# One core, an mLSTM cell and a tanh-shrink layer: fixed instruction order on VectorE and ScalarE, steps placed by their due time

## The chip, the core and the metric

The kernel runs on one core of a Trainium2 chip. TensorE (PE in the profile; its weight loads are PEld) multiplies matrices into PSUM, VectorE (DVE) and ScalarE (ACT) work element by element, GpSimd (POOL) and SyncE (SP) mostly issue DMAs here. Each engine has its own list of instructions, and engines wait for each other by semaphores. The metric is device microseconds of one execution; lower is better.

## The reference

Two blocks in a row, all in float32. The first is an mLSTM cell with batch 4, 8 heads, 768 steps and head size 40; the second is a layer with 320 inputs, 2048 hidden features and 320 outputs.

```python
for t in range(S):
    m_new = np.maximum(f_gate[:, :, t] + m, i_gate[:, :, t])
    f_stab = np.exp(f_gate[:, :, t] + m - m_new)
    i_stab = np.exp(i_gate[:, :, t] - m_new)
    C = f_stab * C + i_stab * outer(v_t, k_t)
    n = f_stab * n + i_stab * k_t
    y[:, :, t] = sigmoid(o_gate[:, :, t]) * (C @ q_t) / max(abs(n . q_t), 1.0)
...
h = x @ w_in
out = (h - np.tanh(h)) @ w_out
```

Here x is y with heads and features joined, 3072 tokens of 320. The two weights come as 64-bit floats and are turned into float32 on the chip.

## The kernel before

**Units.** The cell works on 24 units n of 128 tokens: unit n is chunk c = n // 4 of batch b = n % 4. For a unit, `scores` multiplies keys with queries (PSUM tile ps) and its mask step writes P on VectorE; `prepare` makes the values scaled by the gates (vs), the decayed state, and the sigmoid of o; `inter` and `intra` multiply with state and P into ph; `gate` is five short VectorE operations (den, den, den, o, ys) that divide by the denominator and apply o; `update` multiplies into pc, from which VectorE makes the next state; `turn` transposes ys into px, and ScalarE copies px to xT, the input of the layer. The tiles ph, pc and px of all units take turns in two PSUM banks (`small`, tags b0 and b1); from item 16 or so they share one.

**Pairs and items.** The layer works on groups g of two units (256 tokens) and on eighths p of the hidden features. `up` of a pair (g, p) multiplies xT with w_in and w_rest into one of two PSUM tiles ph_up; `shrink` computes g = h - tanh(h) with a polynomial: on ScalarE z and q, two each, on VectorE four operations gt, of which the first two read ph_up; `down` multiplies gt with w_out into po, and when a run of pairs ends, po is added to a partial sum (part) or becomes the output (ob). For groups 4 to 10 `down_seven` does the same with seven products instead of eight, from sums of gt (s1 to s4, `sums_of_g`) and sums of w_out (wT, `sums_of_weights`), and `put_together` adds the results. The 96 pairs are put in 50 items, two pairs each except four. In item x the program gives: `up` of the item's pairs, then (`halves`) its last third and the scores of a new unit, then `shrink` and the mask steps, then `down` of item x - 1.

**Weights.** `weights` makes of each block of 64-bit weights three steps: `fetch` (a DMA by GpSimd's queue into one of eight buffers w64), `split` (w_e and w_m on VectorE, w_e and w_r on ScalarE) and `join` (three VectorE operations, w_r, w_e and the product that is w_in, w_rest or w_out). Five blocks make one p. The blocks of p = 0 are converted in the prologue by hand. For the others, `due[p]` is the item in which p is first used, less a quarter, with some spacing; `spread_over` lays the blocks of p between due[p-1] and due[p].

**What sets the order.** All matmuls and transposes go through the class `T`, which chains each to the one before, so TensorE follows the program throughout. `Pinned` does the same for VectorE and ScalarE (line 107 issues all their instructions, so the profile shows L107 for them), but only until the prologue ends: `Pinned.on = False` (line 838) leaves `self.last` as it is, and each later instruction is tied only to the last one of the prologue. In the loop over items (line 839) the framework orders VectorE and ScalarE by its own plan, from data dependencies and the order of the program.

**Steps between.** What is not dense work (cell steps, weight steps, the gates of chunks 1 to 5) is laid at points of time, in items, by `spread_over`; `cell_slot` gives the steps of a unit with a cost each, `merge` puts the list of an item between the dense steps. A unit's slot is half an item to 1.5 items wide at the start, about 2.5 from item 7 on. Its last steps are `gate` and `turn` of the unit before; in the single-bank form (`single`) they are `gate`, five pauses, four `update`, four pauses, three `turn` of the same unit, four pauses. The old `merge` takes the list whose share of cost done is smaller:

```python
i = int(done[1] / total[1] < done[0] / total[0])
```

A pause, and `gate`, have the cost 0.

**Gates.** `gates(0, 1)` in the prologue handles chunk 0; `gates(1, NT)` at the start of item 1 handles chunks 1 to 5: a scan and three operations on rows, ten transposes, three matmuls, and exponentials, in one go.

Of the kernel before, what the change touches and what calls it, by code (L numbers as in the profile page):

```python
# [39 lines left out]

# [37 lines left out]
def kernel(  # L78
# [16 lines left out]
    class Pinned:  # L95


        on = True

# [3 lines left out]
        def __getattr__(self, name):  # L103
            method = getattr(self.engine, name)

            def call(*args, **kwargs):
                i = method(*args, **kwargs)  # L107
# [10 lines left out]
    class T:  # L118
# [14 lines left out]
        @classmethod  # L133
        def transpose(cls, *args, **kwargs):
            return cls.keep(nc.tensor.transpose(*args, **kwargs))  # L135

# [147 lines left out]
    def gates(c0, c1, idle):  # L284

        t0, t1, cs, n = c0 * L, c1 * L, slice(c0, c1), c1 - c0
# [11 lines left out]
        cols = []  # L298
        for row in (lf, i_sb):
            p = small([L, NT, BH], "pcol")  # L300
            for c in range(c0, c1):
                T.transpose(p[:, c, :], row[:, c * L:(c + 1) * L], ident[0:BH, 0:BH])
            cols.append(p[:, cs])
        V.tensor_copy(out=lfT[:, cs], in_=cols[0])
        A.activation(out=ei[:, 2, cs], in_=cols[1], func=AF.Exp)
        awake(idle)

        def sums_of(w):
            p = small([w.shape[1], NT, BH], "psum_lf")
# [4 lines left out]
        p = sums_of(upto)  # L314
        V.tensor_single_scalar(inv[:, cs], p, 2 * DEEP, op=OP.max)
        least = sums[:, NG * NP + 2 + (c0 > 0):NG * NP + 3 + (c0 > 0)]
        V.tensor_reduce(out=least, in_=inv[:, cs].rearrange("p c n -> p (c n)"), axis=mybir.AxisListType.X, op=OP.min)
        A.activation(out=inv[:, cs], in_=inv[:, cs], func=AF.Exp, scale=-1.0)
        p = sums_of(after)
        A.activation(out=eS[:, cs], in_=p, func=AF.Exp)  # L320
        awake(idle)
        V.tensor_tensor(out=ei[:, 0, cs], in0=ei[:, 2, cs], in1=inv[:, cs], op=OP.mult)
        V.tensor_tensor(out=ei[:, 1, cs], in0=ei[:, 2, cs], in1=eS[:, cs], op=OP.mult)
        half = sums_of(ones).rearrange("p c (b j two) -> p (c b) two j", two=2, j=HH)
        us = slice(c0 * B, c1 * B)
        A.activation(out=eT[:, us], in_=half[:, :, 1, :], func=AF.Exp)
        A.activation(out=eT[0:D, us], in_=half[0:D, :, 0, :], func=AF.Exp)
        V.tensor_single_scalar(least, least, TINY / DEEP, op=OP.mult)
# [7 lines left out]
    def weights(dst, srcs, queue):  # L336
# [12 lines left out]
        def split():  # L349
            if src.dtype == FP:  # L350
                return
            hi = w["hi"] = w["st"].bitcast(I32).rearrange("p (n two) -> p n two", two=2)[:, :, 1]
            lo = w["st"].bitcast(U32).rearrange("p (n two) -> p n two", two=2)[:, :, 0]
            e, m, r = (conv.tile([128, n], I32, name=name, tag=name, bufs=3)[0:p] for name in ("w_e", "w_m", "w_r"))
            w["e"], w["m"], w["r"] = e, m, r

            V.tensor_single_scalar(e, hi, 0x7FF00000, op=OP.bitwise_and)
            A.activation(out=e, in_=e, func=AF.Relu, scale=8.0, bias=rebias[0:p])

            V.tensor_scalar(out=m, in0=hi, scalar1=0xFFFFF, scalar2=0x41000000, op0=OP.bitwise_and, op1=OP.bitwise_or)  # L360
            A.activation(out=r.bitcast(FP), in_=lo, func=AF.Copy, scale=2.0 ** -52)

        def join():
            if src.dtype == FP:
                return
            e, m, r = w["e"], w["m"].bitcast(FP), w["r"].bitcast(FP)

            V.scalar_tensor_tensor(out=r, in0=m, scalar=-7.0, in1=r, op0=OP.add, op1=OP.add)
            V.scalar_tensor_tensor(out=e, in0=w["hi"], scalar=-(1 << 31), in1=e, op0=OP.bitwise_and, op1=OP.bitwise_or)
            V.tensor_tensor(out=dst, in0=r, in1=e.bitcast(FP), op=OP.mult)  # L370

        return fetch, split, join
# [5 lines left out]
    def convert():  # L378
# [211 lines left out]
    def down_seven(some):  # L590
# [4 lines left out]
        def product(where, a, x, b):  # L595
            bank, block = where
            if g not in pS:
                pS[g] = [ps_o.tile([128, 3, HM], FP, name="pS0", tag="po0"),
# [7 lines left out]
        steps = []  # L606
        for k in range(7):
            for x, (_, p) in enumerate(some):
                even, odd = (w_out[:, 2 * p + i, :].rearrange("p (two n) -> p two n", two=2) for i in range(2))
                a11, a12, a21, a22 = (gT[some][i][:, x, tt * L:(tt + 1) * L] for tt in range(GT) for i in range(2))  # L610
                s1, s2, s3, s4 = (t[:, x] for t in gS[some])
                where, a, b = (
                    ((0, 2), a11, even[:, 0]), ((0, 0), a12, odd[:, 0]), ((2, 1), a22, wT[p][:, 3]),
                    ((1, 1), s3, wT[p][:, 2]), ((1, 0), s1, wT[p][:, 0]), ((0, 1), s2, wT[p][:, 1]),
                    ((2, 0), s4, odd[:, 1]))[k]
# [7 lines left out]
    def put_together(g):  # L623
# [8 lines left out]

        A.copy(out=a, in_=bank[0][:, 2])
        V.tensor_tensor(out=ob[:, 0:5:4], in0=bank[0][:, 0:2], in1=twice(a), op=OP.add)
# [391 lines left out]
```

## Time and profile before

| | |
|---|---|
| median of 3 runs | 679.09 us (677.19 to 679.75) |
| the profiled execution | 679.15 us |
| its span, first to last instruction | 677.4 us |
| TensorE busy | 590.0 us, 3471 instructions |
| VectorE busy | 355.3 us, 888 instructions |
| ScalarE busy | 191.7 us, 483 instructions |
| GpSimd busy | 28.8 us, 60 instructions |
| moved by DMA | 38.23 MB |

The span begins with the first instruction and ends with the last; 1.75 us of the execution lie outside it. A matmul of float32 stands in the trace as two records, so counts of matmuls are twice those of the program. A share of busy time is a mean over stages with different limits. Tile names are those of the program without buffer numbers; "px<-ident,ys" is the transpose of `turn`. In the lists of waits, "PE px <- DVE ys" means that TensorE stood before a transpose into px until VectorE had finished ys: either because it reads ys, or because ys was the last to read the PSUM bank that px takes. A wait is put down to what came last. The granted clock of TensorE is given as a share of full speed.

### The profile page before, as it was taken

The numbers are of one execution on the slowest core, as the hardware profiler recorded it, in microseconds if no ns is written. First come the engines' busy times: TensorE is split into PE (matmuls) and PEld (weight loads), VectorE is DVE, ScalarE is ACT, GpSimd is POOL, SyncE is SP. The second block draws the span as 40 slices with busy tenths as digits, with TensorE's granted clock in tenths as the row PEclk, the third lists the DMA queues.
The fourth block names the chain that finished last, engine by engine and source line by source line (L and its number), as shares of the span: only waits on it lengthen the run. The fifth ranks groups of instructions, "written<-read, shape, count | busy, mean of one in ns | idle before, by whom it ended". The sixth has DMA issues, their size and how long they took to land. (4 is left out here: it accounts for less than half of the span.)

```text
span 677.4 us, 9300 instructions
## 1 busy us (share of the span) xinstructions
PE 590.0 (87%) x3471; PEld 488.9 (72%) x3473; DVE 355.3 (52%) x888; ACT 191.7 (28%) x483; POOL 28.8 (4%) x60
## 2 busy tenths in 40 slices
PE   4974977787989798988998899899989999989996
PEld 2854766575767566766887788688878889878874
DVE  1679878989342623363646346444526345534421
ACT  1342644542212321221331222312223121313321
POOL 2012123100000000000000000000000000000000
PEclk8575676899899989999999799989989899989999
DMA  7644345421110101022111112111100000000000
GB/s 217 191 147 147 102 152 157 135 58 49 30 39 20 40 20 39 21 59 78 59 40 41 38 40 70 38 30 39 30 11 30 1 0 20 1 20 1 19 2 24
DMA packets 40868, 38.23 MB, mean 56 GB/s; under 512 B 3856, under 2 KB 38352, under 8 KB 40816
## 3 DMA queue, kind: packets, MB, share of 16 engines
q1 hardware_dynamic: 33000, 22.82, 11.6%
q0 software_dynamic: 2800, 9.18, 4.5%
q10 hardware_dynamic: 5016, 5.57, 2.4%
q8 instruction: 29, 0.48, 0.3%
q14 instruction: 23, 0.19, 0.1%
HBM read 33.62 MB, written 3.93 MB: 55 GB/s over the span
## 5 line engine op out<-in xcount | busy, mean ns | idle before, releaser
L131 PE MATMUL ph_up<-xT,w_in 128*128 128x256 f32 x768 | 217.5, 412 | 3.2 <-ACT xT L107 3.2
L107 DVE SCALAR_TENSOR_TENSOR gt<-ph_up,z 128x512 f32<-128x512 f32 (+1 forms) x100 | 62.6, 665 | 223.4 <-ACT z L107 223.1
L131 PEld LDWEIGHTS ph_up<-xT,w_in 128*128 128x128 f32 x768 | 142.0, 203 | 18.8 <-ACT xT L107 4.3
L107 ACT ACTIVATE z<-ph_up 128x512 f32<-128x512 f32 (+1 forms) x100 | 57.1, 576 | 271.8 <-issue 137.9
L131 PE MATMUL po<-w_out,gt 128*128 128x320 f32 x320 | 110.5, 469 | 9.5 <-DVE part L107 9.4
L131 PEld LDWEIGHTS ph<-vs,P 128*128 128x128 f32 x384 | 73.7, 219 | 21.1 <-issue 6.2
L131 PEld LDWEIGHTS po<-w_out,gt 128*128 128x128 f32 x320 | 56.9, 201 | 29.7 <-DVE part L107 12.1
L131 PE MATMUL ph<-vs,P 128*128 128x41 f32 x384 | 67.2, 275 | 6.7 <-DVE ys L107 3.7
L107 ACT ACTIVATE q<-z,tiny 128x512 f32<-128x512 f32 (+1 forms) x100 | 64.7, 701 | 0.0
L107 DVE SCALAR_TENSOR_TENSOR gt<-q,gt 128x512 f32<-128x512 f32 (+1 forms) x100 | 62.4, 663 | 0.0
L131 PE MATMUL pS<-wT,s 128*128 128x160 f32 x336 | 60.5, 318 | 0.0
L135 PE MATMUL px<-ident,ys 128*128 128x128 f32 x72 | 20.6, 323 | 43.5 <-DVE ys L107 34.6
L131 PE MATMUL ph_up<-xT,w_rest 64*128 64x256 f32 x384 | 55.5, 406 | 0.0
L131 PEld LDWEIGHTS pS<-wT,s 128*128 128x128 f32 x336 | 51.8, 203 | 0.1
L135 PEld LDWEIGHTS px<-ident,ys 128*128 128x128 f32 x72 | 10.9, 161 | 51.4 <-issue 48.3
L131 PEld LDWEIGHTS ph_up<-xT,w_rest 64*128 64x128 f32 x384 | 33.1, 187 | 14.7 <-issue 11.8
L131 PE MATMUL pS<-w_out,gt 128*128 128x160 f32 x224 | 39.8, 313 | 0.0
L131 PEld LDWEIGHTS ph<-state,q 80*128 80x128 f32 x160 | 30.2, 203 | 7.9 <-ACT xT L107 2.6
L131 PEld LDWEIGHTS pS<-w_out,gt 128*128 128x128 f32 x224 | 31.6, 190 | 4.0 <-issue 3.6
L131 PEld LDWEIGHTS pc<-vs,k 128*80 128x80 f32 x160 | 22.2, 169 | 16.4 <-issue 11.2
L107 DVE TENSOR_TENSOR P<-ps,upto 128x512 f32<-128x512 f32 x48 | 31.6, 684 | 3.4 <-PE ps L131 3.4
L131 PE MATMUL pc<-vs,k 128*80 128x82 f32 x160 | 26.1, 263 | 6.6 <-DVE ys L107 5.6
(92 smaller groups left out, 565.0 us busy)
## 6 DMA issues: line engine op xcount, KB each, us to landing
w<-in_moe_w_out POOLq DMA_DIRECT2D x14, 320.0 KB, 3.3
kz<-in_kT SPq DMA_DIRECT2D x48, 80.0 KB
v<-in_v SPq DMA_DIRECT2D x24, 160.0 KB
k<-in_k SPq DMA_DIRECT2D x24, 160.0 KB
o<-in_o_gate SPq DMA_DIRECT2D x24, 160.0 KB
out<-ob ACTq DMA_DIRECT2D x24, 160.0 KB
qz<-in_qT SPq DMA_DIRECT2D x44, 80.0 KB
q<-in_qT SPq DMA_DIRECT2D x40, 80.0 KB
```

Of the source, the lines that this page charges most:

```text
L107: i = method(*args, **kwargs)
L131: return cls.keep(nc.tensor.matmul(*args, **kwargs))
L135: return cls.keep(nc.tensor.transpose(*args, **kwargs))
```

## The change

VectorE and ScalarE stay pinned in the loop too: each of their instructions is tied to the one before it in the program, so they run in the order of the program. Some operations are then no longer given where their input is started but where it is due: a class `Clock` counts the costs of the steps given so far, `later` holds an operation back until so much has passed, and `need` gives it at once where something depends on it.

- In `shrink`, the four gt are given 0.9 to 3.2 us later, and the sums of g behind them; in `put_together` the additions come 0.5 us behind ScalarE's copy; the DMAs of the output, issued by ScalarE, come 1 or 2 us behind what they send, and are pinned too.
- The conversion of a block becomes fetch, exponent, mantissa, one, sign and product, six single steps that `spread_over` lays one by one; each has the cost 0. In `mantissa` w_r is given before w_m.
- `merge` places a step of an item at its share of the item's dense cost, whatever its own cost.
- `gates` is cut in two: `gate_rows` (scan and three operations), for chunks 1 to 5 now in the prologue behind the scores of unit 2, and `gate_columns`, five steps laid over item 0 from 0.1 to 0.9, with the PSUM banks of po instead of b0 and b1. The loads of these gates move ahead of k and o of the first two units.

```diff
     class Pinned:
-        on = True
...
                 if self.last is not None:
                     tc.add_manual_dep(i.ins, self.last.ins.name, NO_SYNC, reason="order of an engine")
-                if Pinned.on:
-                    self.last = i
+                self.last = i
...
+    class Clock:
+        now, serial, waiting = 0.0, 0, []
+        @classmethod
+        def later(cls, key, wait, step):
+            cls.serial += 1
+            heapq.heappush(cls.waiting, (cls.now + wait, cls.serial, key, step))
+        @classmethod
+        def tick(cls, us):
+            cls.now += us
+            while cls.waiting and cls.waiting[0][0] <= cls.now:
+                heapq.heappop(cls.waiting)[-1]()
+        @classmethod
+        def need(cls, key):
+            while any(entry[2] == key for entry in cls.waiting):
+                heapq.heappop(cls.waiting)[-1]()
...
+    load_gates(later)
     for name in "ko":
         for n in range(2):
             load_unit(n, (name,))
...
-    def gates(c0, c1, idle):
+    def gate_rows(c0, c1):
...
+    def gate_columns(c0, c1, bank):
...
+        return forget, admit, since, until, whole
...
+        def exponent():
+            w["hi"] = w["st"].bitcast(I32).rearrange("p (n two) -> p n two", two=2)[:, :, 1]
+            e = w["e"] = conv.tile([128, n], I32, name="w_e", tag="w_e", bufs=3)[0:p]
+            V.tensor_single_scalar(e, w["hi"], 0x7FF00000, op=OP.bitwise_and)
+            Clock.later(w["st"], 0.6, lambda: A.activation(out=e, in_=e, func=AF.Relu, scale=8.0, bias=rebias[0:p]))
...
         for x in range(len(blocks) + 4):
-            def step(x=x):
-                for late, part in enumerate((0, None, 1, None, 2)):
-                    if part is not None and BLOCK <= x - late < len(blocks):
-                        blocks[x - late][part]()
-            steps.append((1.0, step))
+            block = [blocks[i] if BLOCK <= i < len(blocks) else (lambda: None, (), ()) for i in (x, x - 2, x - 4)]
+            steps.append([block[0][0], *block[2][2], *block[1][1]])
...
             for i in range(2):
-                V.scalar_tensor_tensor(out=gt[i], in0=ph[i], scalar=TINY_POLY[0], in1=z[i], op0=OP.mult, op1=OP.mult)
-            for i in range(2):
-                V.scalar_tensor_tensor(out=gt[i], in0=q[i], scalar=TINY_POLY[2], in1=gt[i], op0=OP.add, op1=OP.mult)
+                Clock.later(some, 0.9 + 0.35 * n * i, lambda i=i: V.scalar_tensor_tensor(
+                    out=gt[i], in0=ph[i], scalar=TINY_POLY[0], in1=z[i], op0=OP.mult, op1=OP.mult))
+                Clock.later(some, 1.0 + 0.75 * n + 0.35 * n * i, lambda i=i: V.scalar_tensor_tensor(
+                    out=gt[i], in0=q[i], scalar=TINY_POLY[2], in1=gt[i], op0=OP.add, op1=OP.mult))
             if some[0][0] in SEVEN:
-                sums_of_g(some)
+                Clock.later(some, 1.01 + 1.1 * n, lambda: sums_of_g(some))
...
     def merge(a, b):
-        total = [sum(cost for cost, _ in x) or 1.0 for x in (a, b)]
-        done, at = [0.0, 0.0], [0, 0]
-        while at[0] < len(a) or at[1] < len(b):
-            i = int(done[1] / total[1] < done[0] / total[0])
...
+        total, done, b = sum(cost for cost, _ in a), 0.0, list(b)
+        for cost, step in a + [(0.0, lambda: None)]:
+            while b and (b[0][0] * total <= done or step is None):
+                _, us, other = b.pop(0)
+                Clock.tick(us)
+                other()
+            Clock.tick(cost)
+            step()
+            done += cost
+        for _, us, other in b:
+            Clock.tick(us)
+            other()
...
     for p in range(1, NP):
-        spread_over(steps[ready[p - 1]:ready[p]], due[p - 1], due[p])
+        spread_over([(0.0, step) for some in steps[ready[p - 1]:ready[p]] for step in some], due[p - 1], due[p])
...
-    load_gates(later)
...
     halves(scores(2))
-    split[3]()
+    gate_rows(1, NT)
+    do(split[3])
...
-    Pinned.on = False
+    spread_over([(0.3, step) for step in gate_columns(1, NT, lambda i, shape: ps_o.tile(shape, FP, name="gate", tag=f"po{i}"))], 0.1, 0.9)
     for x in range(len(items) + LAG):
-        if x == 1:
-            gates(1, NT, 0)
...
-        merge(dense, [(cost, step) for _, cost, step in sorted(work[x], key=lambda w: w[0])])
+        merge(dense, [(at - x, cost, step) for at, cost, step in sorted(work[x], key=lambda w: w[0])])
```

More of the change, by code (lines that the diff above doesn't have):

```diff
@@ L596, in product @@
             bank, block = where
+            if isinstance(a, int):
+                a = gS[some][a][:, x]
             if g not in pS:
+                Clock.need("result")
                 pS[g] = [ps_o.tile([128, 3, HM], FP, name="pS0", tag="po0"),
@@ L604, in product @@
             started[bank] = True
-        steps = []
+        steps = [(0.0, lambda: Clock.need(some))]
         for k in range(7):
@@ L690, in product @@
                 po[tt] = ps_o.tile([128, DM], FP, name="po", tag=f"po{tt}")
+            Clock.need(some)
             T.matmul(po[tt], gT[some][i][:, x, tt * L:(tt + 1) * L], w_out[:, f, :], start=start, stop=stop)
@@ L787, with do @@
     awake(9)
-    gates(0, 1, 2)
+    gate_rows(0, 1)
+    forget, admit, since, until, whole = gate_columns(0, 1, lambda i, shape: small(shape, "gate"))
+    forget()
+    admit()
+    awake(2)
+    since()
+    until()
+    awake(2)
+    whole()
     fetch, split, join = zip(*first)
+    def do(steps):
+        for step in steps:
+            step()
+            Clock.tick(10.0)
     begin(0)
@@ L816 @@
     awake(2)
-    join[1]()
-    split[2]()
+    do(join[1])
+    do(split[2])
     inside(1)
```

136 lines of the change are left out of this document (67 added, 69 removed).

## The prediction, made before the change was run

> **What bounds the kernel now.** I read the busy time of each engine in five stretches first, because the shares of the whole span mix stages with different limits.
>
> ```profile
> span 677.4 us, 9300 instructions
> ```
> ```profile
> core 0: us, PE busy (x) PEld busy (x) DVE busy (x) ACT busy (x) POOL busy (x), PEclk, DMA share, GB/s
> 0.00:38.00 38.00, 26.27 (x139) 18.93 (x141) 17.66 (x61) 8.44 (x22) 6.05 (x19) 0.73 0.66 196
> 38.00:157.00 119.00, 92.57 (x506) 76.56 (x506) 100.81 (x298) 55.21 (x144) 22.76 (x41) 0.76 0.42 126
> 157.00:324.00 167.00, 144.26 (x764) 110.13 (x763) 72.49 (x169) 37.09 (x95) 0.00 (x0) 0.95 0.13 38
> 324.00:661.00 337.00, 316.53 (x2024) 276.46 (x2024) 161.35 (x357) 87.61 (x217) 0.00 (x0) 0.97 0.09 27
> ```
>
> The 38 us at the front are a prologue whose order is already fixed on every engine. From 38 to 157 us VectorE is the fullest engine (100.81 of 119) while TensorE runs at a granted clock of 0.76, so its work is only about 92.57 x 0.76 = 70 us at full speed. From 157 us on TensorE is the bound: 144 of 167 and 317 of 337 us. Next, what TensorE waits for: the waits of that engine alone, one fence each for the second, third and fourth stretch (total, times, longest).
>
> ```profile
> PE px L135 <- DVE ys L107: 16.0, 5, 5.2
> ```
> ```profile
> PE px L135 <- DVE ys L107: 11.9, 4, 4.4
> PE po L131 <- DVE part L107: 8.2, 7, 1.7
> ```
> ```profile
> PE px L135 <- DVE state L107: 8.8, 5, 2.7
> PE px L135 <- DVE ys L107: 6.7, 3, 3.3
> PE pc L131 <- DVE ys L107: 3.7, 3, 2.2
> ```
>
> These are waits for a short result of VectorE, though VectorE is half idle there. The timeline of one of them shows why.
>
> ```profile
> 231.22 1.29 DVE L107 SCALAR_TENSOR_TENSOR gt<-ph_up,z 128x512 f32<-128x512 f32 x2 [2.89 <-ACT z L107]
> ...
> 233.62 1.28 DVE L107 TENSOR_TENSOR P<-ps,upto 128x512 f32<-128x512 f32 x2
> 234.82 0.16 DVE L107 SCALAR_TENSOR_TENSOR den<-ph,inv 128x8 f32<-128x8 f32 x1
> 234.90 0.48 DVE L107 TENSOR_TENSOR part<-po,part 128x320 f32<-128x320 f32 x1
> ...
> 235.36 0.82 DVE L107 TENSOR_TENSOR vs<-v,ei 128x640 f32<-128x640 f32 x1
> ...
> 236.85 0.49 DVE L107 TENSOR_TENSOR ys<-ph,o 128x320 f32<-128x320 f32 x1
> ...
> 237.49 0.45 PE L135 MATMUL px<-ident,ys 128*128 128x128 f32 x1 [4.14 <-DVE ys L107]
> ```
>
> The five operations of `gate` (den to ys) run from 234.82 to 237.34, 2.5 us, of which part and vs, put between them, take 1.3; alone they would take 1.2 us. They begin only behind gt, a second pair of gt and P (231.22 to 234.90); `turn` has been given so close behind that TensorE stands 4.14 us. A stall also costs clock (stretches as above):
>
> ```profile
> 199.70:201.60 1.90, 0.00 (x0) 0.01 (x1) 1.67 (x5) 0.00 (x0) 0.00 (x0) 1.00 0.19 37
> 202.00:205.20 3.20, 3.20 (x9) 2.51 (x8) 0.00 (x0) 0.47 (x1) 0.00 (x0) 0.50 0.17 51
> ```
>
> After 1.9 us of silence TensorE got half its clock for at least 3.2 us. The Trainium skill ("TensorE: Matmul & The Clock Gate", Part 1) puts the return to half speed after an idle window of about 3.4 us; by that, stalls under that length would cost no clock, and the two clock terms below would nearly vanish (13 us less gain). The row speaks against it, and the sum goes by the row.
>
> **The change, part by part.**
>
> (a) *Weight conversion held to its place.* One group of w (five blocks) is an eighth of these rows of VectorE:
>
> ```profile
> L107 DVE SCALAR_TENSOR_TENSOR w_e<-w,w_e 128x256 int32<-128x256 int32 (+2 forms) x40 | 16.6, 414 | 0.0
> L107 DVE SCALAR_TENSOR_TENSOR w_r<-w_m,w_r 128x256 f32<-128x256 f32 (+2 forms) x40 | 16.5, 413 | 0.3 <-ACT w_r L107 0.3
> L107 DVE TENSOR_SCALAR w_e<-w 128x256 int32<-128x256 int32 (+2 forms) x40 | 11.3, 283 | 0.0
> L107 DVE TENSOR_SCALAR w_m<-w 128x256 int32<-128x256 int32 (+2 forms) x40 | 11.3, 282 | 0.0
> L107 DVE TENSOR_TENSOR w_out<-w_r,w_e 128x320 f32<-128x320 f32 x16 | 7.7, 482 | 0.1
> L107 DVE TENSOR_TENSOR w_in<-w_r,w_e 128x256 f32<-128x256 f32 x16 | 6.6, 412 | 0.1
> L107 DVE TENSOR_TENSOR w_rest<-w_r,w_e 128x128 f32<-128x128 f32 x8 | 2.3, 282 | 0.0
> ```
>
> Sum 72.3, a group 9.0 us. The places come from `due`: 0.5, 1.75, 3.75, 5.75, 7.5, 8.75 and 11.75 items for groups 1 to 7. The view of the tile w_out and the groups of VectorE from 38 to 157 us say where they ran:
>
> ```profile
> L107 DVE TENSOR_TENSOR w_out<-w_r,w_e x16: 477/481/493, 38.9 to 156.3; 128x320 f32<-128x320 f32 x16
> ```
> ```profile
> L107 DVE SCALAR_TENSOR_TENSOR gt<-ph_up,z 128x256 f32<-128x256 f32 (+1 forms) x12 | 6.4, 556 | 16.2 <-ACT z L107 16.2
> L107 DVE SCALAR_TENSOR_TENSOR gt<-q,gt 128x256 f32<-128x256 f32 (+1 forms) x12 | 6.3, 555 | 0.0
> ```
>
> The last block is done at 156.3 us, when only six items (12 gt, two an item) have passed: nothing holds VectorE to the program in the loop, and groups 5 to 7 ran up to six items early, in the stage where VectorE is the bound. In program order these 3 x 9.0 = 27 us leave the stretch, whose VectorE work falls to about 73, beside TensorE's 70. What is it then worth? At best the stretch runs at the ratio of now, 119/100.8, over 73: 86 us. At worst VectorE's idle time (16.2 us before gt) only grows and 119 stays. I take the middle, 102: both engines now wait in turn for each other, and half clock will not go. Gain 17 us, less 4 for (d): 13.
>
> The 27 us come back in items 6 to 12. There VectorE has 5 to 7 us of conversion an item beside gt (2.6), its share of the cell (vs, P, state and gate, near 5 us a unit, a unit in 1.5 to 2.5 items) and a part or two, 11 to 13 us, against 10.9 us that an item of the fourth stretch takes (337 us, 31 items); items 6 to 8 are over by some 2 us each. Cost 7 us. The sums of w_out, too, are now held to their place:
>
> ```profile
> L107 DVE TENSOR_TENSOR wT<-w_out 128x160 f32<-128x160 f32 x16 | 4.8, 318 | 0.0
> ```
>
> With the other 16 like them that is 10 us in items 18 to 22, in lumps of four (1.3 us), beside gt and s. From 0 (idle VectorE takes them) to 6 us (half of them in front of something due); I take 2.
>
> (b) *`merge` puts steps where they are due.* The old merge went by cost, so `gate` and the pauses (cost 0) made no distance; now a step stands at its share of the item. From item 19 a unit has 33 steps over about 2.5 items of 10.9 us, 0.8 us a step: six steps, 5 us, from `gate` to the first `update`, five from the last `update` to `turn`. A chain of 1.2 us behind at worst four gt (2.6) fits. Of the 19.2 us of waits in the fourth stretch 17 go, and of its clock loss, (1 - 0.97) x 337 = 10 us, 8. Before that (third stretch) a unit has 20 steps over 2.5 items, and only two, 2.4 us, from the last `intra` to `turn`: of the 11.9 us a third stays, gain 8. The part waits (8.2) come from gt pairs in front of the eviction; spaced, one gt (0.66) at most is in front, and two products (0.54 us each by the program's own cost) cover it: 6. Clock: of (1 - 0.95) x 167 = 8.4 us, 5.
>
> (c) *gt given 0.9 to 3.2 us after the item's end, s behind it; masks P in front.* Cost nothing, as long as gt has read the bank before the next item's first matmul. The chain of waits has the cover:
>
> ```profile
> 618.88 4.00 PE pS L131 x28
> 622.88 4.52 PE ph_up L131 x24
> ```
>
> These 4.0 us of pS, and the cell's products, stand between. P (1.28) and two gt (1.29) need 2.6 of them after the scores. If the cover went, each us late would cost a us an item, 50 items.
>
> (d) *Later gates.* The scan and three operations move into the prologue:
>
> ```profile
> L107 DVE TENSOR_TENSOR_SCAN xT<-xT,xT,xT 32x640 f32<-32x640 f32 x1 | 1.5, 1529 | 0.0
> L107 DVE TENSOR_TENSOR xT<-xT,xT 32x640 f32<-32x640 f32 x3 | 2.4, 809 | 0.0
> ```
>
> 3.9 us of VectorE in front of the conversions that item 0 needs; I count them in full, as nothing there covers them. Leaving item 1 they free the px wait of 5.2 us there (already in (a)). The two loads (32 x 640 x 4 B each, 164 KB, 0.8 us at the 196 GB/s of the first stretch) go ahead of k and o on SP's queue; k's first reader is the first `update`, behind the whole of unit 0, and o is read later still: 0, or 0.8 us if that cover goes. The transposes change banks and place, not count: 0, bounds -1 to +3 for the chain in item 0.
>
> (e) *Fixed order on ScalarE, out DMAs included.* ScalarE is under half full everywhere; -1 to +4, I take 0. The swap of w_m and w_r: 0.
>
> Sum: second stretch 13, third 8 + 6 + 5 - 7 = 12, fourth 17 + 8 - 2 = 23; 48 us. 677.4 - 48 = 629, plus 1.75 outside the span (the profiled execution took 679.15, the median is 679.09): **631 us**.
>
> **Rivals.**
>
> *A, the early stage gives nothing.* VectorE and TensorE work in lockstep at half clock, and what (a) saves returns in items 6 to 8: for it, the clock of 0.76 with TensorE idle only 22%; against it, 27 us less work. Without the 13 us of the second stretch it is 644; with only two thirds of the 44 us of (b) besides, 659.
>
> *B, slower: the wrong thing in front.* With a fixed order a VectorE operation whose input is late stops everything behind it, gt above all, and gt frees the two up banks. Place: between an item's end and the next item's first matmul. Against it: gt needs 2.6 of 4.0 us. It decides once gt is late by 1 us beyond that cover in each of 50 items (50 us against the 48); at 1.4 us it is 679 - 48 + 70 = 701. The Trainium skill says the queues of VectorE and ScalarE are strictly first in, first out ("TensorE: Matmul & The Clock Gate", Part 1, on the engines' queue depths); by that the chip would not repair such an order. The trace of before shows no operation that is late in this way.
>
> *C, the order hardly changes.* If VectorE already runs nearly in program order, 679. The conversions at 156 us speak against it, as does `part` between two `den`.
>
> *D, stalls cost no clock.* If the half clock of the last two stretches comes from something other than the stalls, the 8 and 5 us stay lost: 644. Against it: it follows the silence of 1.90 us directly, and the clock was 1.00 until then. The Trainium skill's idle window, cited above, would come out here.
>
> **Chances.** Forecast (613 to 646) 0.55, A beyond that (to 670) 0.25, D 0.04, C 0.06, B 0.10. The forecast's own ends: (a) at 86 and wT at 0 give 613; (b) at two thirds 646. The range takes in A at two thirds and the unknowns of (d) and (e), and below the forecast's end some 7 us for the 7 of items 6 to 8: 606 to 664. A measurement of this kernel can tell about 0.5% from no change; faster by more than that 0.84, within it 0.06, slower 0.10.
>
> **What would show it.** The last w_out conversion at about item 11 instead of 156 us; VectorE under 80 us in the time of items 0 to 5; no px or pc waits above 1 us after item 19, granted clock 1.00 there; part waits under 2 us in all; pS waiting on wT around items 18 to 22 if (a) costs more. I am wrong if TensorE waits for gt or z, or if items 0 to 8 take as long as before.

## The result, and the profile after

| | median us (range) | ratio to before, 95% interval |
|---|---|---|
| before, 4 runs beside it | 679.35 (677.19 to 679.75) | |
| after, 4 runs | 620.46 (616.0 to 623.15) | 0.9133 [0.9076, 0.9189] |

The change makes the kernel 8.7% faster. The profiled execution of after took 616.0 us, the shortest of its four; the stages below are cut from it, so their sum, 63.1 us, is a little more than the 58.9 between the medians. First the head of the page of after. The counts of instructions are those of before or close to them; TensorE is busy for 25.6 us less, VectorE for 9.4 more.

```profile
span 614.3 us, 9270 instructions
...
PE 564.4 (92%) x3473; PEld 472.7 (77%) x3473; DVE 364.7 (59%) x888; ACT 188.7 (31%) x483; POOL 28.2 (5%) x60
```

To compare stages, both traces are cut at the same work: at the first z of items 0, 5, 18 and 49 (the z that ScalarE takes from an item's first finished `up`), and once more from item 1 to item 5. The windows of before, columns as in the prediction (busy time and count of each engine, granted clock, DMA share, GB/s):

```profile
49.10:149.40 100.30, 77.44 (x432) 64.20 (x432) 86.58 (x256) 47.01 (x120) 20.07 (x36) 0.75 0.41 124
149.40:323.90 174.50, 151.09 (x808) 115.49 (x807) 79.61 (x190) 40.38 (x104) 0.00 (x0) 0.95 0.14 40
323.90:662.60 338.70, 318.23 (x2034) 277.46 (x2035) 161.45 (x357) 87.74 (x218) 0.00 (x0) 0.97 0.09 26
```

The same three of after:

```profile
54.10:137.00 82.90, 67.04 (x418) 55.94 (x418) 54.15 (x150) 28.75 (x77) 9.19 (x17) 0.84 0.33 99
137.00:293.50 156.50, 146.35 (x810) 112.37 (x807) 101.10 (x256) 52.90 (x137) 9.69 (x18) 0.98 0.23 67
293.50:599.40 305.90, 305.90 (x2034) 271.60 (x2035) 176.03 (x386) 88.66 (x225) 0.00 (x0) 1.00 0.10 30
```

Items 0 to 4 take 17.4 us less, items 5 to 17 18.0, items 18 to 48 32.8; the first z comes 5.0 us later. In the last row TensorE is busy for 305.90 of 305.90 us at full clock: there nothing but less work would help. VectorE's 86.58 us in the first row have become 54.15, and the 79.61 in the second 101.10: the conversions moved back. The waits of TensorE over the whole of after (total, times, longest), three rows of the list:

```profile
PE px L133 <- DVE ys L106: 18.7, 9, 3.0
...
PE ph_up L129 <- ACT xT L106: 6.7, 3, 5.6
...
PE po L129 <- DVE part L106: 1.0, 3, 0.4
```

The part waits are down to 1.0 us, and all px waits left lie before item 18. The long wait of ph_up for xT, 5.6 us once, is new. The table gives every profiled execution of this study cut in the same way (us; starts of z in each trace).

| | first z of item 0 | item 0 | items 1-4 | 5-8 | 9-17 | 18-48 | rest | span |
|---|---|---|---|---|---|---|---|---|
| before | 49.1 | 30.9 | 69.4 | 58.6 | 115.9 | 338.7 | 14.9 | 677.4 |
| after | 54.1 | 24.1 | 58.8 | 46.6 | 110.0 | 305.8 | 14.9 | 614.3 |
| e1, loop free | 55.2 | 24.8 | 59.3 | 52.0 | 102.3 | 305.8 | 14.8 | 614.1 |
| e2, old merge | 55.1 | 22.2 | 62.6 | 47.9 | 109.1 | 320.9 | 15.0 | 632.9 |
| e3, before pinned | 48.8 | 31.0 | 71.5 | 63.8 | 119.8 | 368.7 | 14.9 | 718.6 |
| e4, before + merge | 48.0 | 30.7 | 67.0 | 54.4 | 106.7 | 309.3 | 14.8 | 631.0 |
| e5, gt at once | 54.8 | 25.2 | 67.1 | 55.1 | 120.2 | 311.0 | 14.8 | 648.2 |
| e6, blocks whole | 56.6 | 23.1 | 61.9 | 48.4 | 108.6 | 305.8 | 14.9 | 619.3 |
| e7, gates back | 49.1 | 28.6 | 61.0 | 46.6 | 108.2 | 305.8 | 15.2 | 614.5 |
| e8, turn later | 55.7 | 22.3 | 61.3 | 46.1 | 103.1 | 305.8 | 14.9 | 609.4 |
| e9, free, gt at once | 55.2 | 26.3 | 69.6 | 54.0 | 105.9 | 309.3 | 15.1 | 635.4 |
| e10, free, turn later | 54.7 | 24.6 | 59.7 | 44.3 | 101.7 | 305.8 | 15.1 | 605.9 |
| e11, e7 + e8 | 49.4 | 27.9 | 61.3 | 46.1 | 103.1 | 305.8 | 15.1 | 608.6 |
| e12, e11 + other queue | 41.8 | 28.2 | 59.9 | 46.1 | 103.1 | 305.8 | 15.4 | 600.3 |

There is one trace of each kernel, and two runs of one kernel may differ by some us (after's four span 7 us), so single differences of 1 or 2 us in the early columns are not read.

### The profile page after: what moved, and what is told of

Read it like the earlier page. It is cut to its first block, busy times and chain, and to the rows that moved or that the text cites. A ratio compares the mean times of both kernels' runs of the same rounds, so it can differ in the third digit from the quotient of the medians.

```text
span 614.3 us, 9270 instructions
## 1 busy us (share of the span) xinstructions
PE 564.4 (92%) x3473; PEld 472.7 (77%) x3473; DVE 364.7 (59%) x888; ACT 188.7 (31%) x483; POOL 28.2 (5%) x60
## 4 chain that ended last, share of the span: by engine, by line
PE 82%; DVE 12%; DMA 2%; issue 1%; ACT 1%; ACTq 0%; SPq 0%; DVEq 0%
PE ph_up L129 37%; PE pS L129 19%; PE po L129 11%; PE ph L129 8%; PE ps L129 4%; DVE gt L106 2%; PE pc L129 2%; DVE P L106 2%; PE px L133 2%; DMA kz<-in_kT 1%; PE awake L129 1%; DVE o L106 1%; DVE den L106 1%; DVE w_e L106 1%; DVE ys L106 1%
## 5 line engine op out<-in xcount | busy, mean ns | idle before, releaser
L129 PE MATMUL ph_up<-xT,w_in 128*128 128x256 f32 x768 | 206.8, 398 | 6.7 <-ACT xT L106 6.7
L129 PEld LDWEIGHTS ph_up<-xT,w_in 128*128 128x128 f32 x768 | 135.7, 194 | 20.4 <-ACT xT L106 7.2
L129 PE MATMUL po<-w_out,gt 128*128 128x320 f32 x320 | 107.7, 459 | 1.4 <-DVE part L106 1.0
L106 DVE TENSOR_TENSOR P<-ps,upto 128x512 f32<-128x512 f32 x48 | 30.9, 686 | 75.8 <-PE ps L129 75.8
L129 PE MATMUL ph<-vs,P 128*128 128x41 f32 x384 | 65.5, 266 | 6.1 <-DVE vs L106 3.1
L129 PEld LDWEIGHTS po<-w_out,gt 128*128 128x128 f32 x320 | 55.4, 196 | 18.9 <-DVE part L106 3.5
L129 PE MATMUL pS<-wT,s 128*128 128x160 f32 x336 | 56.3, 304 | 0.0
L129 PEld LDWEIGHTS pS<-wT,s 128*128 128x128 f32 x336 | 48.0, 190 | 0.0
L106 ACT ACTIVATE w_e<-w_e,rebias 128x256 int32<-128x256 int32 (+2 forms) x40 | 20.3, 508 | 74.0 <-DVE w_e L106 73.9
L133 PE MATMUL px<-ident,ys 128*128 128x128 f32 x72 | 19.1, 291 | 19.5 <-DVE ys L106 18.7
L129 PEld LDWEIGHTS ph<-state,q 80*128 80x128 f32 x160 | 28.5, 195 | 6.5 <-issue 1.3
L129 PEld LDWEIGHTS ps<-qz,kz 40*128 40x128 f32 x384 | 28.9, 211 | 2.3 <-DVE P L106 0.8
L133 PEld LDWEIGHTS px<-ident,ys 128*128 128x128 f32 x72 | 10.2, 147 | 26.2 <-issue 22.2
```

The costliest lines, as they stand in the source:

```text
L129: return cls.keep(nc.tensor.matmul(*args, **kwargs))
```

## The experiments

Every ratio is to the kernel before, timed beside it, and kernels are compared with each other by these ratios.

**e1: the fixed order taken out of after's loop.** VectorE and ScalarE are pinned to the end of the prologue only; due times, single steps, merge and gates stay.

```diff
+        on = True
...
-                self.last = i
+                if Pinned.on:
+                    self.last = i
...
+    Pinned.on = False
     for x in range(len(items) + LAG):
```

> The changed kernel, but VectorE and ScalarE free in the loop again (tied only to the prologue); due times and the new merge stay. Theory of the prediction: the late stretch keeps its gain, because that comes from where the steps stand in TensorE's order: items 18 to 49 take 306 to 312 us (before 338.7, after 305.9). The conversions run early again, so the last w_out conversion is done by about item 6 and items 0 to 5 take about 100 us as before (after 82.9). Time 632 to 645 us. Rival 'the fixed order does it all': items 18 to 49 go back to about 338 us and the time is 665 to 680. Rival 'placement does it all': 615 to 623, as after.

617.4 us (615.34 to 620.21), 0.9105 [0.9066, 0.9144]: no different from after. The fixed order by itself is worth nothing that can be measured. The last addition to w_out stands in the view of that tile (count, min/median/max ns, first and last start) for after, then for e1:

```profile
L106 DVE TENSOR_TENSOR w_out<-w_r,w_e x16: 478/491/493, 41.5 to 249.8; 128x320 f32<-128x320 f32 x16
```
```profile
L108 DVE TENSOR_TENSOR w_out<-w_r,w_e x16: 476/482/493, 42.6 to 150.0; 128x320 f32<-128x320 f32 x16
```

In e1 the conversions run early again, as in before, and items 1 to 4 still take 59.3 us against 58.8. So holding them to their place is not what made the early stage shorter.

**e2: the old merge in after.** Steps go by cost again; a step of the conversion is weighed as a sixth of its block, so the places are those of the old form only nearly.

```diff
-        total, done, b = sum(cost for cost, _ in a), 0.0, list(b)
+        weigh = lambda cost: 1.0 / 6 if cost == 0.001 else cost
+        total = [sum(weigh(cost) for cost, _ in x) or 1.0 for x in (a, b)]
...
+            i = int(done[1] / total[1] < done[0] / total[0])
...
-        spread_over([(0.0, step) for some in steps[ready[p - 1]:ready[p]] for step in some], due[p - 1], due[p])
+        spread_over([(0.001, step) for some in steps[ready[p - 1]:ready[p]] for step in some], due[p - 1], due[p])
```

> The changed kernel with the old merge by cost (a block of weights counts 1.0 as before, a sixth for each step); fixed order and due times stay. Theory: the waits of TensorE for px and pc come back in the late stretch, which takes 332 to 340 us (after 305.9); conversions keep their place, so items 0 to 5 stay near 83 to 92 us. Time 642 to 662 us. Rival 'the fixed order does it all': 615 to 625.

636.4 us (634.25 to 638.38), 0.9381 [0.9344, 0.9418]: by the ratios 17 us of the gain go, and 15.1 are lost in items 18 to 48. The waits of its TensorE from 291 to 620 us show px and pc waiting for ys once more:

```profile
PE px L133 <- DVE ys L106: 5.9, 4, 1.6
PE pc L129 <- DVE ys L106: 3.9, 3, 1.6
```

**e3: the fixed order alone, in before.**

```diff
-    Pinned.on = False
     for x in range(len(items) + LAG):
```

> The kernel before with one line taken out, so that VectorE and ScalarE stay in program order in the loop; gt given at once, blocks converted whole, old merge. Theory: conversions are held to their place (last w_out after item 11) and items 0 to 5 gain 5 to 17 us of 100, but the late stretch keeps its waits or adds to them, as gt stands at VectorE's head: 335 to 350 us. Time 660 to 685 us. Rival 'the fixed order does it all': 615 to 635.

720.23 us (715.83 to 721.04), 1.0591 [1.0547, 1.0634]: slower by 41 us, 30 of them in items 18 to 48. The waits of its TensorE, whole run:

```profile
PE px L135 <- DVE ys L107: 31.1, 11, 5.0
PE po L131 <- DVE part L107: 16.1, 10, 3.3
PE px L135 <- DVE state L107: 13.5, 5, 4.2
```

And its timeline of VectorE in one item (start, duration, line, operation, tiles, idle time before it and what ended it):

```profile
481.60 1.29 DVE L107 SCALAR_TENSOR_TENSOR gt<-ph_up,z 128x512 f32<-128x512 f32 x2 [10.78 <-ACT z L107]
...
482.81 1.28 DVE L107 SCALAR_TENSOR_TENSOR gt<-q,gt 128x512 f32<-128x512 f32 x2
...
484.01 0.75 DVE L107 TENSOR_TENSOR s<-gt 128x256 f32<-128x256 f32 x2
...
485.60 1.28 DVE L107 TENSOR_TENSOR P<-ps,upto 128x512 f32<-128x512 f32 x2
...
487.65 0.17 DVE L107 SCALAR_TENSOR_TENSOR den<-ph,inv 128x8 f32<-128x8 f32 x1 [0.78 <-PE ph L131]
```

VectorE sits idle for 10.78 us because the next operation in the program is a gt whose z is not there, and then everything due comes at once. gt, s and P take 5.3 us here, from 481.60 to 486.88, before anything short gets its turn. The banks of `up` are not what waits: TensorE stands for ys, part and state, the short results behind that row of long ones.

**e4: the new merge alone, in before.**

```diff
-        total = [sum(cost for cost, _ in x) or 1.0 for x in (a, b)]
-        done, at = [0.0, 0.0], [0, 0]
...
+        total, done, b = sum(cost for cost, _ in a), 0.0, list(b)
+        for cost, step in a + [(0.0, lambda: None)]:
+            while b and (b[0][0] * total <= done or step is None):
...
-        merge(dense, [(cost, step) for _, cost, step in sorted(work[x], key=lambda w: w[0])])
+        merge(dense, [(at - x, cost, step) for at, cost, step in sorted(work[x], key=lambda w: w[0])])
```

> The kernel before with the new merge alone; VectorE and ScalarE free in the loop, gt given at once, blocks whole. Theory: the late stretch gains nearly all, 306 to 314 us (before 338.7); items 0 to 5 stay near 100 us, the last w_out conversion at about 156 us. Time 632 to 648 us. Rival 'the fixed order does it all': 670 to 680. Rival 'only both together': above 660 in this run and in the three others.

633.65 us (632.7 to 638.56), 0.9357 [0.9314, 0.94]: three quarters of the gain, from placement in `merge` alone, without any fixed order. Items 18 to 48 take 309.3 us.

**e5: gt and its sums given at once, in after's fixed order.**

```diff
             for i in range(2):
-                Clock.later(some, 0.9 + 0.35 * n * i, lambda i=i: V.scalar_tensor_tensor(
-                    out=gt[i], in0=ph[i], scalar=TINY_POLY[0], in1=z[i], op0=OP.mult, op1=OP.mult))
...
+                V.scalar_tensor_tensor(out=gt[i], in0=ph[i], scalar=TINY_POLY[0], in1=z[i], op0=OP.mult, op1=OP.mult)
+            for i in range(2):
+                V.scalar_tensor_tensor(out=gt[i], in0=q[i], scalar=TINY_POLY[2], in1=gt[i], op0=OP.add, op1=OP.mult)
...
-                Clock.later(some, 1.01 + 1.1 * n, lambda: sums_of_g(some))
+                sums_of_g(some)
```

> The changed kernel with one part undone: the four gt and the sums behind them are given at once in shrink, still in fixed order. Theory H (gt at VectorE's head, waiting for ScalarE, is what made the fixed order alone slower, 720 us): items 18 to 49 rise from 305.8 to 325 us or more, part waits come back, time 640 to 680. Rival (the old merge, which gave the short chains no distance, did it; gt at once costs nothing): items 18 to 49 within 304 to 310 us, time 614 to 626. On the early gain: if due times of gt brought it, items 1 to 5 go from 58.8 back to 66 to 70 us.

648.25 us (646.43 to 651.22), 0.9553 [0.9501, 0.9605]: by the ratios 28 us worse than after, 8.3 us of it in items 1 to 4 (67.1), the rest spread over all stages. In the fixed order, giving gt where it is due is worth more than the whole early stage of the prediction.

**e9: the same in a free loop** (the edits of e1 and e5 together).

> As e1 (VectorE and ScalarE free in the loop), and the four gt and the sums given at once. Theory G (the due times of gt brought the early gain, with or without a fixed order): items 1 to 5 go from 59.3 back to 66 to 70 us and the time is 628 to 638, near the 634 of the old kernel with the new merge. Rival (in a free order the place of gt does not matter, since the planner fills around it; single steps and moved gates brought the early gain): items 1 to 5 at 58 to 61, time 614 to 622. Against e5 (648, same places in fixed order) it also gives the price of the fixed order when gt stands at VectorE's head.

637.06 us (633.87 to 637.12), 0.9363 [0.9328, 0.9398]: by the ratios 18 us worse than e1, and equal to e4. It is 13 us better than e5, which differs from it only by the fixed order: with gt at once, that order costs 2%, also with the new merge. The windows of items 1 to 4 for five kernels, in the order before, after, e1, e9, e5:

```profile
80.00:149.40 69.40, 56.44 (x326) 45.91 (x325) 59.50 (x177) 32.15 (x83) 13.08 (x23) 0.85 0.41 121
```
```profile
78.20:137.00 58.80, 48.97 (x325) 39.60 (x323) 38.28 (x102) 20.57 (x55) 5.39 (x10) 0.97 0.31 93
```
```profile
80.00:139.30 59.30, 50.37 (x323) 40.61 (x323) 56.40 (x167) 30.76 (x80) 14.32 (x25) 0.94 0.47 144
```
```profile
81.50:151.10 69.60, 60.46 (x324) 48.37 (x323) 57.14 (x171) 30.99 (x81) 12.66 (x22) 0.77 0.41 119
```
```profile
80.00:147.10 67.10, 58.99 (x325) 47.28 (x325) 39.39 (x103) 20.69 (x55) 5.54 (x10) 0.81 0.27 82
```

Read VectorE first. After and e5 have the same 38 to 39 us of it and differ by 8.3 us in length; after and e1 differ by 18 us of it and have the same length; e1 is 95% full (56.40 of 59.30) and still short. So VectorE's load does not set this stage. Then TensorE: its busy time times its clock is 48, 48, 47, 47 and 48 us, the same work each time within 1.5, and its idle time is 13.0, 9.8, 8.9, 9.1 and 8.1. e9 and e5, with gt at once, do not idle longer than e1 and after; they run at a lower clock. The column of items 1 to 4 in the table says the same of all traces: the nine kernels with due times for gt take 58.8 to 62.6 us there, the five without 67.0 to 71.5. In the second view of the page, 40 slices of some 16 us, the half clock of item 0 lasts longer. After, then e9:

```profile
PEclk7575589999999899999999999999999999999999
```
```profile
PEclk8585558879899999999999999999999999999998
```

After's sixth slice (77 to 92 us) has 0.8, and the seven behind it 0.9 or more; e9's sixth (79 to 95 us) still has half clock, and the next three stay below 0.9. What the due times change in the order is in the timelines of VectorE around one gt, after first (item 2):

```profile
96.32 1.29 DVE L106 TENSOR_TENSOR P<-ps,upto 128x512 f32<-128x512 f32 x2 [6.93 <-PE ps L129]
...
97.92 0.67 DVE L106 SCALAR_TENSOR_TENSOR state<-pc,own,state 80x164 f32<-80x164 f32 x2
...
98.92 1.28 DVE L106 SCALAR_TENSOR_TENSOR gt<-ph_up,z 128x512 f32<-128x512 f32 x2
...
100.52 0.15 DVE L106 SCALAR_TENSOR_TENSOR den<-ph,inv 128x8 f32<-128x8 f32 x1
...
101.66 0.49 DVE L106 TENSOR_TENSOR ys<-ph,o 128x320 f32<-128x320 f32 x1
...
102.07 0.68 DVE L106 SCALAR_TENSOR_TENSOR gt<-q,gt 128x512 f32<-128x512 f32 x1
```

e9, the same place:

```profile
104.30 1.29 DVE L108 SCALAR_TENSOR_TENSOR gt<-ph_up,z 128x512 f32<-128x512 f32 x2 [3.99 <-ACT z L108]
105.50 1.28 DVE L108 SCALAR_TENSOR_TENSOR gt<-q,gt 128x512 f32<-128x512 f32 x2
106.70 1.28 DVE L108 TENSOR_TENSOR P<-ps,upto 128x512 f32<-128x512 f32 x2
...
108.89 0.15 DVE L108 SCALAR_TENSOR_TENSOR den<-ph,inv 128x8 f32<-128x8 f32 x1
...
111.05 0.48 DVE L108 TENSOR_TENSOR ys<-ph,o 128x320 f32<-128x320 f32 x1
```

In after P and state, which TensorE wants within the item, go ahead of gt, and the chain from den to ys goes ahead of the second pair of gt; from the first of these operations to the end of ys it takes 5.8 us. In e9 four gt stand in front of all of it: 7.2 us. gt itself is read only by `down`, which the program gives an item later. That this order is what brings the higher clock in items 1 to 4 is not shown. From item 5 to 17 the waits show its use directly: there TensorE waits for part 9.0 us in e9 and 2.6 in e1.

**e6: the steps of a weight block given together again.**

```diff
-        spread_over([(0.0, step) for some in steps[ready[p - 1]:ready[p]] for step in some], due[p - 1], due[p])
+        spread_over([(0.0, lambda some=some: [step() for step in some]) for some in steps[ready[p - 1]:ready[p]]], due[p - 1], due[p])
```

> The changed kernel with one part undone: the steps of a weight block are given together, at the place where the first would stand. Theory S (single steps brought the gain of items 1 to 5, 69.4 to 58.8 us): these items go back to 66 to 71 us and the time is 626 to 640. Rival (due times of gt, or the moved gates, brought it): items 1 to 5 stay at 57 to 61, time 614 to 626.

621.4 us (619.53 to 627.35), 0.9182 [0.9118, 0.9246]: the intervals overlap. Giving the steps singly shows no effect.

**e7: the gates of chunks 1 to 5 back in item 1,** in one go, their loads back behind the prologue's unit 1.

```diff
-    load_gates(later)
     for name in "ko":
...
     do(join[2])
+    load_gates(later)
...
-    gate_rows(1, NT)
...
-    spread_over([(0.3, step) for step in gate_columns(1, NT, lambda i, shape: ps_o.tile(shape, FP, name="gate", tag=f"po{i}"))], 0.1, 0.9)
     for x in range(len(items) + LAG):
+        if x == 1:
+            gate_rows(1, NT)
+            for step in gate_columns(1, NT, lambda i, shape: small(shape, "gate")):
+                step()
```

> The changed kernel with the later gates as before: loads behind the first units, rows and columns at once at the start of item 1, in banks b0 and b1. The prediction counted 4 us for the rows in the prologue: the first z comes at 49 to 50 us (after 54.1), and the 4 us of VectorE come back in front of item 1's turn, item 0 to 1 at 29 to 31 us (after 24.1). Time within 617 to 627 us. If the spacing of the gates is what helped items 1 to 5, those rise above 62 us and the time above 627.

616.44 us (615.71 to 618.47), 0.9094 [0.9054, 0.9134]: the intervals overlap again. The first z comes 5.0 us earlier, item 0 takes 4.5 us longer. Where after loses most of the 5.0 us stands in its timeline of the prologue:

```profile
35.13 1.53 DVE L106 TENSOR_TENSOR_SCAN xT<-xT,xT,xT 32x640 f32<-32x640 f32 x1
...
36.69 2.40 DVE L106 TENSOR_TENSOR xT<-xT,xT 32x640 f32<-32x640 f32 x3
...
39.02 0.31 DVE L106 TENSOR_SCALAR w_e<-w 128x320 int32<-128x320 int32 x1
...
39.36 0.56 ACT L106 ACTIVATE w_e<-w_e,rebias 128x320 int32<-128x320 int32 x1 [6.77 <-DVE w_e L106]
...
40.20 0.46 ACT L106 COPY xT<-px 128x384 f32<-128x384 f32 x1
...
40.72 1.22 PE L129 MATMUL ph_up<-xT,w_in 128*128 128x256 f32 x2 [5.58 <-ACT xT L106]
```

The rows of the gates hold back VectorE's w_e, that holds back ScalarE's w_e, and the copy to xT stands behind it in ScalarE's order, though VectorE has no part in the copy: TensorE stands 5.58 us before the first `up`. That `up` starts at 40.72 us, and at 37.75 in e7: 3.0 us come by this path. The other 2.0 lie between it and the first z, where after's TensorE also does ten transposes of the gates, 1.5 us together.

**e8: more distance from the last `intra` to `turn`.** Units of the early form, in two banks, get four pauses there and one at the end.

```diff
-        return steps + turning
+        return steps + 4 * [(0.0, lambda: None)] + turning + [(0.0, lambda: None)]
```

> The changed kernel with four pauses between gate and turn, and one behind, in the two-bank form of a unit, so that turn stands some 4 steps further behind gate. If the remaining px waits (18.7 us, 9 times, two of them followed by half clock) are distance alone, they fall below 8 us, items 0 to 18 lose 10 to 15 us of 239, and the time is 603 to 612. Rival (VectorE is too far behind at this place, so the wait only moves, or ph of the next unit waits for xT instead): 614 to 626.

608.22 us (606.77 to 611.11), 0.8959 [0.8921, 0.8996]: 12 us faster than after, the intervals apart. Its px waits:

```profile
PE px L133 <- DVE ys L106: 8.3, 4, 3.2
```

They fall from 18.7 us in 9 to 8.3 in 4. The four left lie before item 5; in items 5 to 17, where after has 7.8 us in five, none is left, and items 9 to 17 fall from 110.0 to 103.1. The part waits rise from 1.0 to 4.1 us. The two traces differ by 4.9 us only, since the execution of after is the shortest of its four and that of e8 the longest; so they show where some 7 of the 12 us come from, and not the rest. One of the stalls that go is at 208 us in after (windows of after):

```profile
208.00:210.80 2.80, 0.00 (x1) 0.00 (x0) 2.66 (x9) 2.05 (x5) 0.00 (x0) 0.88 0.22 66
211.00:216.80 5.80, 5.80 (x13) 3.71 (x14) 4.94 (x11) 0.99 (x2) 0.00 (x0) 0.50 0.15 47
```

2.8 us without a matmul, then 5.8 us at half clock, a loss of 2.8 + 2.9 us. VectorE is busy for 2.66 of the 2.80: this stall, in the stage to which the conversions came back, is made of work ahead of ys, and pauses cover it.

**e10: e8 in a free loop** (edits of e1 and e8).

> As e8 (turn further behind gate), VectorE and ScalarE free in the loop. If the fixed order is worth nothing once the steps are well placed, 604 to 612, as e8 (608). If it has a worth that e1 hid (conversions that run early make the waits of units worse), above 613.

608.52 us (607.1 to 610.96), 0.8968 [0.8933, 0.9003]: equal to e8. Once steps and due times are right, the fixed order neither costs nor brings anything, here as in e1.

**e11: e7 and e8 together.**

> As e8, with the later gates as before the change, as in e7. If the two gains add (12 us of e8, 4 of e7), 602 to 608 and the first z at 49 us. If e7's 4 us were the same stalls, 606 to 612.

608.95 us (607.58 to 610.36), 0.8958 [0.8929, 0.8987]: e8 and no more. Against e8 the first z comes 6.3 us earlier, and item 0 takes 5.6 of them, much as in e7.

**e12: e11, and all fetches of weights from GpSimd's queue** in place of ScalarE's.

```diff
-            queue = nc.gpsimd if p else A
+            queue = nc.gpsimd
```

> As e11, and the first five weight blocks are fetched by GpSimd's queue instead of ScalarE's, which is held by issues until 12.7 us while TensorE stands 7.7 us for its first exponential. If the issues alone hold it, the first z comes 4 to 7 us earlier than in e11 and the time falls by as much. Rival: the DMA queues are full (SyncE's issues wait at the same time), or the weights come later by GpSimd, and the time is within 2 us of e11 or above.

602.31 us (601.08 to 608.6), 0.8893 [0.8835, 0.895]: the lowest median of all, and well below before and after; its interval still touches that of e11. ScalarE's first instructions, e11 and then e12:

```profile
4.71 6.76 ACTq L106 DMA_DIRECT2D w<-in_moe_w_in  x5
12.61 0.82 ACTq L106 DMA_DIRECT2D w<-in_moe_w_out  x2
13.46 1.28 ACT L106 ACT_TABLE_LOAD   x1 [13.46 <-DMA w<-in_moe_w_in]
```
```profile
4.66 1.28 ACT L106 ACT_TABLE_LOAD   x1 [4.66 <-issue]
```

In e11 ScalarE issues seven DMAs of weights from 4.71 to 13.4 us and computes nothing; in e12 it starts at 4.66, and the first z comes at 41.8 us in place of 49.4.

## Why the prediction was right, and where it was not

The forecast of 631 us lay 10.5 us above the median, and the range held it. The sum was nearly right as a sum of other parts, and that is partly luck: in (a) the number came out by another mechanism, and (c), put at nothing, was worth 18 us. Ordered by the ratios, the gain builds up so: before 1; the new merge (e4) 0.9357; with single conversion steps, moved gates and the delays of `put_together` and of the output as well (e9) 0.9363; with due times for gt (e1) 0.9105; with the fixed order (after) 0.9133. So merge brings some 44 us, the due times 18, and the rest nothing that can be measured. The two overlap: without the new merge after loses 17 us (e2), not 44.

**(a) Conversions held to their place: the number came out, the reason fell.** 17 us were predicted, items 0 to 4 gained 17.4, and the last w_out moved; but 6.8 of the 17.4 lie in item 0, and 4.5 of these are the gates' (e7). And e1 has the conversions early, and its items 1 to 4 are as short. The step that failed is "the stage where VectorE is the bound": a VectorE that is 95% full does not lengthen it (e1). In items 1 to 4 after gains 10.6 us on before, 3.1 of idle time and 7.5 of busy time at a lower clock. What brings them, as far as the runs go, are the due times of gt: without them 69.6, with them 59.3 (e9, e1). How they raise the clock is open, and after's 58.8 is the lowest of the nine kernels that have them, so some of the 7.5 may be luck (see the last section). Nor did the half clock stay through items 1 to 4, as the working had it. The places were also read too early: by the code groups 1 to 7 are due from item 0.75 to 14.75, not from 0.5 to 11.75, and the last w_out ran in item 14.

The 7 us of cost "in items 6 to 12" came, later: items 9 to 17 take 110.0 in after and 102.3 in e1, 7.7 more. But items 5 to 8 take 46.6 against 52.0, with 1.2 us of px waits against 4.6; net 2.3. The sums wT, held to 289 to 325 us, cost nothing: there TensorE never stands.

**(b) Merge: right, and larger.** For items 18 to 48 the prediction had 23 us, measured 32.8: all waits went and the clock came to 1.00, about 10 us of it, since (1 - 0.97) x 338.7 is 10. e4 shows that placement alone does 29.4 of it. In the third stretch, about items 5 to 17, 12 us were predicted net and 18.0 came. The part waits fell to 1.0 us. That part of the px waits would stay in the third stretch was right in kind, but not a third of them: 7.8 of 12.6 us did (items 5 to 17). The distance to `turn` was too short there, and e8 closed it for 12 us more.

**(c) gt given later: "cost nothing" was the wrong side of zero.** Here the prediction asked only whether gt would be late for the banks, and not what stands behind gt when it is early. It had seen one such case, the part waits, and counted 6 us for it under (b). The due times are worth 18 us in the free order (e9 against e1) and 28 in the fixed one (e5 against after).

**(d) Gates: 4 us predicted, 5.0 seen in the first z,** but 3.0 of it by a path the working did not have, through ScalarE's order and the copy to xT. And item 0 gave them back (24.1 against 28.6 in e7), so that the part is worth about nothing. The loads cost nothing, though k's issue went from 8.7 to 13.7 us and not by 0.8: its reader is later still.

**(e) ScalarE's fixed order: 0 predicted.** Not tried alone; with VectorE's together it is 0 in the loop (e1, e10).

**Rivals.** A (nothing from the early stage) fell with the 17.4 us as a forecast, but what it said of (a) held: moving the conversions gave nothing (e1). D (stalls cost no clock) fell with the clock of 1.00 in items 18 to 48. C fell with the conversions' move. B, slower by a fixed order, is what the fixed order does alone: e3 took 720 us, where 701 were forecast for B. Its place was wrong: not the banks of `up`, but the short results behind gt. Due times are what turned it off, which the prediction did not see: it costed the fixed order's harm and gt's due times as two unrelated parts.

What stays open: why the half clock of the first item lasts until 77 us in after and until 95 and 99 in e5 and e9. The idle times of the stage do not tell them apart, and no run took this by itself. The place of gt alone does not decide it: before and e4, with gt at once, have the full clock again at 79 and 78 us, e7 and e10, with due times, only at 85 and 87. That the conversions are what makes items 9 to 17 longer in fixed order is shown for one stall only (e8), and why items 5 to 8 have fewer px waits in after than in e1 was not found.

## What to carry to other kernels

Where a bound engine waits for short results of one that is half idle, place the steps by distance in time first; here that gave three quarters of the gain, and pauses before the transposes another 12 us. A fixed order on an engine is neither good nor bad by itself: with long operations given where their inputs start it costs 6% with the old merge and 2% with the new one; with each given where its reader needs it, the framework's own order does as well. And a full engine is no proof of a bound: before costing its load, look at which of its operations the stage waits for.

## What the runs showed of the hardware

A stall of 2 us can be enough to halve the clock. In e8 TensorE does next to nothing for 2.00 us and then has half clock for 3.4 us (windows of e8), as it had in before after 1.90:

```profile
104.10:106.10 2.00, 0.06 (x2) 0.06 (x1) 2.00 (x5) 0.00 (x0) 0.36 (x1) 1.00 0.42 123
106.40:109.80 3.40, 3.40 (x12) 2.86 (x12) 1.14 (x4) 0.61 (x2) 0.00 (x0) 0.50 0.42 145
```

But it does not always do so. In items 1 to 4 after and e7 have the same stall at the same place of the program: TensorE stands 3.02 us before a px, until 102.30 us in after and until 102.23 in e7. The 3 us behind it, after and then e7:

```profile
102.30:105.30 3.00, 2.15 (x11) 1.51 (x12) 3.00 (x7) 0.95 (x3) 0.32 (x1) 1.00 0.44 131
```
```profile
102.30:105.30 3.00, 3.00 (x10) 2.32 (x11) 2.63 (x6) 0.95 (x3) 0.00 (x0) 0.50 0.44 129
```

After keeps the full clock and e7 gets half of it. So the length of such a stall does not by itself decide what it costs, and a few us of clock in one trace are no merit of its kernel.

And being busy did not always bring the full clock back: in after TensorE was busy, by the profile's records, for 12.60 of 12.60 us and stayed at 0.50.

```profile
44.20:56.80 12.60, 12.60 (x62) 10.71 (x62) 6.54 (x21) 5.99 (x15) 1.26 (x3) 0.50 0.36 105
```

The Trainium skill ("TensorE: Matmul & The Clock Gate", Part 1) has the full clock return after about 3.4 us of sustained work; this row shows a stretch nearly four times as long without it. Last, issuing DMAs took ScalarE's own time: five issues filled 6.76 us of it in e11. The two behind them took 0.82 together, so an issue has no fixed price here; the runs do not show whether the five waited for something.
